# One shared, block-by-block transpose of the attention weights P in a two-stream diffusion block

## The chip, the cores and the metric

The kernel runs on one core of a Trainium2 chip. Its time is the device time of one execution in microseconds (us). Matrix products and transposes run on TensorE (PE in the profile, with its weight loads as PEld), row-wise arithmetic on VectorE (DVE) and ScalarE (ACT), some small work and DMA issues on GpSimd (POOL), and most DMA issues on SyncE (SP). TensorE writes its results to PSUM, and DVE and ACT move them from there to SBUF.

## The reference

Two batches (B = 2) have 256 image tokens and 32 text tokens each, with width D = 1152. Both streams are normalised, scaled and shifted by rows made from `c`; then follow q, k, v products with weights of their own, one attention over the joined 288 tokens of a batch, an output product, a gate and a residual:

```
hi = _layernorm(x_img) * (1 + sci) + shi          # ht the same with the text weights
qi, ki, vi = split(hi @ wqkv_img)                 # qt, kt, vt = split(ht @ wqkv_txt)
q = concat([qt, qi]); k = concat([kt, ki]); v = concat([vt, vi])
scores = einsum('bqd,bkd->bqk', q, k) * D ** -0.5
p = softmax(scores)
a = einsum('bqk,bkd->bqd', p, v)                  # at = a[:, :32], ai = a[:, 32:]
out_i = x_img + gai * (ai @ wo_img)
out_t = x_txt + gat * (at @ wo_txt)
```

## The kernel before

The order on each engine is the order in which the kernel writes its instructions (`keep_in_program_order`), so what stands first in the code is queued first. Semaphores between the engines are placed by the framework. The last third of the kernel, with which the change has to do, runs as follows.

**Scores and softmax.** For each batch and each 128-row image query tile there is one score tile of 128 x 288 (queries x keys, image keys in columns 0 to 255, text keys in 256 to 287). The text queries of both batches share one tile of 64 rows: rows 0 to 31 are batch 0, rows 32 to 63 batch 1. `soft_max`, `soft_exp` and `soft_div` turn a score tile into P, which DVE writes in bf16 into `pb` (L604). A `pb` tile is 384 columns wide. GpSimd writes a second copy of the 32 text-key columns at columns 320 to 351 (L605), so that after the transpose the text keys stand in more than one 32-row group; unused columns are zero.

**Transposes.** The product with V needs P with the keys on the partitions. `p_transposes` (L628) lets PE transpose 128 x 128 pieces of `pb` into a PSUM tile `pT_ps`, and one copy per PSUM tile brings them to `pT` in SBUF. There are three key blocks `kj`: 0 and 1 are image keys, 2 holds the text keys. Each batch has its own `pT`, of 3 x 288 columns. Each batch transposes its two image query tiles and also the shared text tile; for batch 1 a second permutation matrix, `ident2`, puts batch 1's text queries in front. That is 3 pieces x 3 key blocks x 2 batches = 18 transposes. `pT_ps` comes from the PSUM pool `ps_tr` (2 buffers) for the image key blocks and from `ps_mm` (6 buffers) for the text block. The order is: batch 0 blocks 0 and 1 (one ACT copy of 576 columns), batch 0 block 2 (DVE copy of 288), batch 1 block 2 (DVE copy of 288), batch 1 blocks 0 and 1 (ACT copy of 576). DVE also has `v_txt_out` (L519, L521), which finishes the text rows of V, ahead of its two copies.

**Attention.** `attn_pair` is called three times, each time with three 128-wide column blocks of D for each batch. It takes three accumulators of 128 x 288 for batch 0 (t0) and three for batch 1 (t1) from the six `ps_mm` buffers. `attn_keys` adds the two image key blocks for t0, then six short products with the 32 text keys go to t0 and t1 in turn, then `attn_keys` adds the image key blocks for t1. `attn_evac` (L652 on DVE, L654 on ACT, in turn) adds a bias and writes `aT`. In `attn_keys` the loop is by accumulator: key blocks 0 and 1 of one accumulator, then the next accumulator.

**Output.** `out_img` multiplies `aT` with `w_o_i` in chunks of 384 columns, one `ps_mm` buffer each; DVE multiplies by the gate rows `gb` (L719) and adds the residual (L720). `gb` comes by way of DRAM: ACT copies the gate rows to SBUF (L538), POOL issues a write to a scratch tensor (L540), and then a load that spreads it over 128 partitions (L554). POOL's L540 stands behind L605 in POOL's queue.

Of the kernel before, what the change touches and what calls it, by code (L numbers as in the profile page):

```python
# [9 lines left out]
ALU = mybir.AluOpType  # L10
# [4 lines left out]
def kernel(  # L15
# [14 lines left out]
    nc = tc.nc  # L30
    bf = mybir.dt.bfloat16
# [3 lines left out]
    B, NI, D = x_img.shape  # L35
    NT = x_txt.shape[1]
    P = 128
    KT = D // P
    NTOK = NI + NT
    NIT = (B * NI) // P  # L40
    TPB = NI // P
# [10 lines left out]
    const = ctx.enter_context(tc.tile_pool(name="const", bufs=1))  # L52
    work = ctx.enter_context(tc.tile_pool(name="work", bufs=2))
    small = ctx.enter_context(tc.tile_pool(name="small", bufs=4))
    ps_mm = ctx.enter_context(tc.tile_pool(name="ps_mm", bufs=6, space=PSUM))
    ps_tr = ctx.enter_context(tc.tile_pool(name="ps_tr", bufs=2, space=PSUM))

    pin = tc.keep_in_program_order

    def mm(*a, **k):  # L60
        return pin(nc.tensor.matmul(*a, **k))  # L61

    def tr(*a, **k):
        return pin(nc.tensor.transpose(*a, **k))  # L64
# [63 lines left out]
    ident = const.tile([P, P], bf)  # L128
# [13 lines left out]
    PBW = 3 * P  # L142
# [5 lines left out]
    nc.gpsimd.memset(pb_txt, 0.0)  # L148
    nc.gpsimd.memset(xn_t[NTT:P, (KT - KH) * P:KH * P], 0.0)
    nc.gpsimd.memset(pb_all[:, 0:2 * B, NTOK:PBW], 0.0)  # L150
    ident2 = const.tile([P, P], bf)
    nc.gpsimd.tensor_copy(ident2[:, 0:P - NT], ident[:, NT:P])
    nc.gpsimd.tensor_copy(ident2[:, P - NT:P], ident[:, 0:NT])
    fold = const.tile([P, NGG, LW], bf)
    nc.vector.reduce_max(fold[:, 0, :], ident[:].rearrange("p (g l) -> p l g", g=NGG), axis=AX.X)
    nc.gpsimd.tensor_copy(fold[:, 1:NGG, :], fold[:, 0, :].unsqueeze(1).to_broadcast([P, NGG - 1, LW]))
# [120 lines left out]
    v_i = act.tile([P, NIT, D], bf, tag="A")  # L277
# [83 lines left out]
    for kt in range(KT):  # L361
        for b in range(B):
            h = hT_i[:, kt, b * NI:(b + 1) * NI]
            if b == 0 or kt % 3 == 0:
                nc.vector.tensor_scalar(h, h, sc1_i[:, kt, b:b + 1], sh_i[:, kt, b:b + 1],
                                        op0=ALU.mult, op1=ALU.add)
# [141 lines left out]
    def v_txt(r):  # L508
        ps = ps_mm.tile([P, VC], f32, tag="mm")
        for kt in range(KT):  # L510
            for g in range(2):
                for b in range(B):
                    c0, r0 = g * HD + r * VC, 64 * g + NT * b
                    mm(ps[r0:r0 + NT, :], lhsT=hT_t[:, kt, NT * b:NT * b + NT], rhs=w_v_t[:, kt, c0:c0 + VC],
                       start=(kt == 0), stop=(kt == KT - 1), tile_position=(0, r0))
        return ps

    def v_txt_out(r, ps):
        pin(nc.vector.tensor_sub(v_t[:, r * VC:(r + 1) * VC], ps[:], svb[:, r * VC:(r + 1) * VC]))  # L519
        if r == 0:  # L520
            pin(nc.vector.tensor_sub(v_t[0:NTT, HD:HD + NTT], ps[NTT:P, 0:NTT], svb[NTT:P, 0:NTT]))  # L521
# [30 lines left out]
    def img_gate_spread():  # L552
        for b in range(B):
            pin(nc.gpsimd.dma_start(gb[:, b, :], gsc[0, b, :].partition_broadcast(P)))  # L554
        for g in range(2):
            pin(nc.gpsimd.dma_start(xf[64 * g:64 * g + NTT, :, :],
                                    xt_flat.rearrange("t (r g j) -> g t r j", r=2, g=2)[g]))
# [24 lines left out]
    qpos = [[0, P, 2 * P], [NT, NT + P, 0]]  # L582

    pbs = {}
# [15 lines left out]
    def soft_div(key):  # L600
        sps, qn, nmx, e, rs = soft[key]
        pin(nc.vector.reciprocal(rs[0:qn, :], rs[0:qn, :]))  # L602
        pb = pb_txt if key == "t" else pb_tiles[key[0] * TPB + key[1]]
        pin(nc.vector.tensor_scalar_mul(pb[0:qn, 0:NTOK], e[0:qn, :], rs[0:qn, :]))  # L604
        pin(nc.gpsimd.tensor_scalar(pb[0:qn, NI + 2 * NT:NI + 3 * NT], e[0:qn, NI:NTOK], rs[0:qn, :], 0.0,  # L605
                                     op0=ALU.mult, op1=ALU.add))
        pbs[key] = pb

    def scores_img(b, qi):
# [13 lines left out]
                   start=(ft < 2), stop=(ft >= KT - 2), tile_position=(0, r0))  # L623
        return sps

    pTs = {}

    def p_transposes(b, kjs, pool, copy):  # L628
        pT_ps = pool.tile([P, 8 * P], bf, tag="tr" if pool is ps_tr else "mm", name="pT_ps")
        txt = [(2, pbs["t"], ident2 if b else ident)]  # L630
        img = [(qi, pbs[(b, qi)], ident) for qi in range(TPB)]
        for n, kj in enumerate(kjs):
            for qi, pb, perm in (txt + img if b else img + txt):
                o = n * NTOK + qpos[b][qi]
                k0 = kj * P - (NT * b if kj == 2 else 0)
                tr(pT_ps[:, o:o + P], pb[:, k0:k0 + P], perm[:])
        if b not in pTs:
            pTs[b] = work.tile([P, 3, NTOK], bf, tag="pT", name="pT")
        pin(copy(pTs[b][:, kjs[0]:kjs[-1] + 1, :],  # L639
                 pT_ps[:, 0:len(kjs) * NTOK].rearrange("p (k n) -> p k n", n=NTOK)))  # L640

    def attn_keys(tiles, first):
        for b, dt in tiles:
            for kj in range(2):
                mm(tiles[(b, dt)][:], lhsT=v_i[:, b * TPB + kj, dt * P:(dt + 1) * P], rhs=pTs[b][:, kj, :],
                   start=(first and kj == 0), stop=(not first and kj == 1))

    def attn_evac(tiles):
        for b, dt in tiles:
# [7 lines left out]
    def attn_pair(ids0, ids1):  # L657
        t0 = {key: ps_mm.tile([P, NTOK], f32, tag="mm", name="aps") for key in ids0}
        attn_keys(t0, True)
        t1 = {key: ps_mm.tile([P, NTOK], f32, tag="mm", name="aps") for key in ids1}  # L660
        for n, key in enumerate([x for pair in zip(t0, t1) for x in pair]):
            first, (b, dt) = key in t1, key
            r0, vcols = v_txt_cols(b, dt)
            mm((t1 if first else t0)[key][:], lhsT=vcols,
               rhs=pTs[b][r0:r0 + NT, 2, :], start=first, stop=not first, tile_position=(r0, 0))
        attn_evac(t0)
        attn_keys(t1, False)
        attn_evac(t1)
# [9 lines left out]
    soft_exp(I[0])  # L678
    soft_max(I[1], sp[I[1]], P)
    soft_div(I[0])  # L680
    soft_exp(I[1])
    soft_max(I[2], sp[I[2]], P)
    soft_div(I[1])
    soft_exp(I[2])
    soft_max(I[3], sp[I[3]], P)
    soft_div(I[2])
    pin(nc.scalar.copy(half[:], st[NTT:P, :]))
    soft_exp(I[3])
# [5 lines left out]
    gate_row()  # L694
    v_txt_out(0, vt[0])
    vt.append(v_txt(1))
    p_transposes(0, (0, 1), ps_tr, nc.scalar.copy)
    v_txt_out(1, vt[1])
    p_transposes(0, (2,), ps_mm, nc.vector.tensor_copy)
    p_transposes(1, (2,), ps_mm, nc.vector.tensor_copy)  # L700
    p_transposes(1, (0, 1), ps_tr, nc.scalar.copy)
    img_gate_spread()
    for dts in ((0, 5, 1), (6, 2, 7), (3, 8, 4)):
        attn_pair(*[[(b, dt) for dt in dts] for b in range(B)])
# [73 lines left out]
```

## Time and profile before

| what | value |
|---|---|
| median of 5 runs | 117.56 us (117.33, 117.47, 117.56, 117.80, 118.17) |
| profiled execution | 117.33 us |
| its span in the profile | 115.5 us |
| PE busy | 110.8 us (96%), 1081 matmuls and transposes |
| DVE / ACT / POOL busy | 72.0 / 44.1 / 12.4 us |
| granted TensorE clock | 1.0 |

Times inside the profile count from the start of the span. The profiled execution is 1.8 us longer than its span, and what lies around the span is taken as unchanged. In a group of instructions the columns are line, engine, operation, output<-inputs, shapes and count, then busy time and mean duration of one in ns, then idle time of the engine before them and what ended it. In a timeline a row is start, duration, engine, line, operation, output<-inputs, count, and in brackets the idle time before it; several equal instructions in a row are merged.

### The profile page before, as it was taken

The numbers are of one execution on the slowest core, as the hardware profiler recorded it, in microseconds if no ns is written. First come the engines' busy times: TensorE is split into PE (matmuls) and PEld (weight loads), VectorE is DVE, ScalarE is ACT, GpSimd is POOL, SyncE is SP. The second block draws the span as 40 slices with busy tenths as digits, with TensorE's granted clock in tenths as the row PEclk, the third lists the DMA queues.
The fourth block names the chain that finished last, engine by engine and source line by source line (L and its number), as shares of the span: only waits on it lengthen the run. The fifth ranks groups of instructions, "written<-read, shape, count | busy, mean of one in ns | idle before, by whom it ended". The sixth has DMA issues, their size and how long they took to land.

```text
span 115.5 us, 2586 instructions
## 1 busy us (share of the span) xinstructions
PE 110.8 (96%) x1081; PEld 63.5 (55%) x1081; DVE 72.0 (62%) x152; ACT 44.1 (38%) x92; POOL 12.4 (11%) x34
## 2 busy tenths in 40 slices
PE   4999999999999999999999999999999999999990
PEld 1246644445674444445454457887866556656670
DVE  3479691072959999999995040028758509566571
ACT  5799800050852389735241233334557400100000
POOL 7300000000000000000000000003431600416000
PEclk9999999999999999999999999999999999999999
DMA  3999999999999999999999999999999999952223
GB/s 104 379 385 382 392 404 412 412 413 411 412 397 412 312 396 403 414 410 412 410 364 391 412 405 410 414 407 409 416 402 407 405 417 373 407 190 50 103 51 102
DMA packets 18917, 41.02 MB, mean 355 GB/s; under 512 B 1323, under 2 KB 1851, under 8 KB 18907
## 3 DMA queue, kind: packets, MB, share of 16 engines
q1 hardware_dynamic: 18032, 39.85, 89.9%
q0 software_dynamic: 480, 0.89, 2.2%
q10 hardware_dynamic: 395, 0.12, 0.5%
q8 instruction: 8, 0.13, 0.4%
q14 instruction: 2, 0.02, 0.0%
HBM read 39.52 MB, written 1.34 MB: 354 GB/s over the span
## 4 chain that ended last, share of the span: by engine, by line
PE 83%; DMA 9%; SPq 2%; DVE 2%; ACT 1%; issue 0%
PE ps L61 53%; PE vps L61 15%; DMA t<-in_wqkv_img_dram 9%; PE gps L61 5%; PE aps L61 5%; PE sps L61 4%; SPq L108 2%; DVE tmp L719 1%; DVE o L720 1%; SPq L104 1%; ACT pT L639 1%; PE pT_ps L64 0%; PE tpt L64 0%; PE shps L61 0%
## 5 line engine op out<-in xcount | busy, mean ns | idle before, releaser
L61 PE MATMUL ps<-xT_i,t 128*128 128x512 bf16 x162 | 35.7, 379 | 0.0
L61 PEld LDWEIGHTS <-t 128*128 128x128 bf16 x333 | 20.9, 98 | 19.2 <-issue 0.7
L453 DVE SCALAR_TENSOR_TENSOR acc_sh<-t,sTf,acc_sh 128x1152 f32<-128x1152 bf16 x16 | 21.4, 1404 | 0.0
L61 PE MATMUL ps<-t,aT 128*128 128x384 bf16 (+3 forms) x153 | 20.3, 308 | 0.0
L61 PE MATMUL vps<-t,hS_i 128*128 128x512 bf16 (+1 forms) x108 | 17.9, 326 | 0.1
L61 PEld LDWEIGHTS <-aT 128*128 128x128 bf16 (+1 forms) x153 | 13.0, 101 | 7.1 <-issue 0.8
L61 PEld LDWEIGHTS <-hS_i 128*128 128x128 bf16 x108 | 8.9, 98 | 8.9 <-DVE hS_i L272 0.6
L383 ACT CAST qkT<-ps 128x512 bf16<-128x512 f32 (+2 forms) x11 | 6.1, 551 | 14.8 <-PE ps L61 13.5
L719 DVE TENSOR_TENSOR tmp<-ps,gb 128x384 bf16<-128x384 f32 (+2 forms) x13 | 6.8, 525 | 7.5 <-PE ps L61 3.8
L605 POOL TENSOR_SCALAR pb<-e,rs 128x32 bf16<-128x32 f32 (+1 forms) x5 | 2.2, 445 | 75.5 <-DVE rs L602 75.5
L61 PE MATMUL wps<-warm 128*128 128x512 bf16 x24 | 8.2, 505 | 1.5 <-DVE unit L127 1.5
L381 ACT ACTIVATE qkT<-ps 128x512 bf16<-128x512 f32 (+2 forms) x11 | 6.0, 559 | 8.3 <-PE ps L61 6.7
L180 DVE CAST v_i<-vps 128x512 bf16<-128x512 f32 x5 | 3.5, 691 | 7.9 <-PE vps L61 7.9
L590 DVE TENSOR_REDUCE nmx<-sps 128x1 f32<-128x288 f32 x4 | 1.8, 458 | 9.4 <-PE sps L61 9.4
L182 ACT CAST v_i<-vps 128x512 bf16<-128x512 f32 x4 | 2.3, 580 | 10.0 <-PE vps L61 10.0
L61 PEld LDWEIGHTS <-warm 128*128 128x128 bf16 x25 | 2.7, 119 | 5.5 <-issue 3.0
L652 DVE TENSOR_SCALAR aT<-aps,svc 128x288 bf16<-128x288 f32 x9 | 4.3, 518 | 2.2 <-PE aps L61 2.2
L61 PEld LDWEIGHTS <-sT 128*32 128x32 bf16 x180 | 4.5, 96 | 1.8 <-issue 1.2
L61 PE MATMUL sps<-qkT 128*128 128x288 bf16 (+1 forms) x54 | 5.3, 287 | 0.0
L61 PE MATMUL gps<-t,sT 128*32 128x288 bf16 x144 | 5.2, 287 | 0.0
L61 PE MATMUL aps<-pT,v_i 128*128 128x288 bf16 x36 | 5.1, 287 | 0.1
L61 PE MATMUL ps<-hT_t,t 128*128 128x64 bf16 x162 | 5.0, 193 | 0.0
(114 smaller groups left out, 105.6 us busy)
## 6 DMA issues: line engine op xcount, KB each, us to landing
t<-in_wqkv_txt_dram SPq DMA_DIRECT2D x3, 2592.0 KB, 20.1
t<-in_wmod_img_dram SPq DMA_DIRECT2D x2, 2592.0 KB, 14.3
t<-in_wmod_txt_dram SPq DMA_DIRECT2D x2, 2592.0 KB, 19.7
t<-in_wqkv_img_dram SPq DMA_DIRECT2D x3, 864.0 KB, 13.5
t<-in_wqkv_img_dram SPq DMA_DIRECT2D x1, 2592.0 KB
t<-in_wo_img_dram SPq DMA_DIRECT2D x3, 864.0 KB, 10.9
t<-in_wqkv_img_dram SPq DMA_DIRECT2D x3, 576.0 KB, 10.5
t<-in_wmod_txt_dram SPq DMA_DIRECT2D x2, 864.0 KB, 13.0
```

The source lines that it names most:

```text
L61: return pin(nc.tensor.matmul(*a, **k))
L104: nc.sync.dma_start(x_i[:, b * TPB:(b + 1) * TPB, :], x_img[b].rearrange("(p t) d -> p t d", t=TPB))
L108: nc.sync.dma_start(w_sc_i[:, r0:r1, :], sc_v[:, r0:r1, :])
L180: nc.vector.tensor_copy(out_ap, in_ap)
L182: nc.scalar.copy(out_ap, in_ap)
L381: nc.scalar.mul(out_ap, in_ap, SCALE)
L383: nc.scalar.copy(out_ap, in_ap)
L453: pin(nc.vector.scalar_tensor_tensor(acc, w_sh_t[:, kt, :], col, acc, op0=ALU.mult, op1=ALU.add))
L590: pin(nc.vector.reduce_max(nmx[0:qn, :], sps[0:qn, :], axis=AX.X, negate=True))
L605: pin(nc.gpsimd.tensor_scalar(pb[0:qn, NI + 2 * NT:NI + 3 * NT], e[0:qn, NI:NTOK], rs[0:qn, :], 0.0, op0=ALU.mult, op1=ALU.add))
L652: nc.vector.tensor_scalar(dst, tiles[(b, dt)][:], bias, None, op0=ALU.add)
L719: nc.vector.tensor_mul(tmp[:, 0:n], ps[:, 0:n], gb[:, b, c0:c0 + n])
```

## The change

The text tile is transposed once for both batches. One `pT` of 3 x 576 columns holds both: batch 0's two image tiles, batch 0's text, batch 1's text, batch 1's image tiles. A PSUM tile now holds one key block for both batches, so there are three of them (blocks 0 and 1 from `ps_tr`, block 2 from `ps_mm`) and 15 transposes, ordered by key block, all with `ident`. `ident2` goes. For the text tile GpSimd writes its text-key columns three times over (64 x 96 in place of 64 x 32). All 15 transposes are queued ahead of the copies: ACT copies block 0 of batch 0, block 1 of batch 0 and block 1 of batch 1 (288 columns each); DVE copies block 0 of batch 1 (288) and then block 2 of both batches (576). On the t0 side `attn_keys` now goes by key block: block 0 of all three accumulators, then block 1 of all three.

```diff
-    ident2 = const.tile([P, P], bf)
-    nc.gpsimd.tensor_copy(ident2[:, 0:P - NT], ident[:, NT:P])
-    nc.gpsimd.tensor_copy(ident2[:, P - NT:P], ident[:, 0:NT])
...
-        pin(nc.gpsimd.tensor_scalar(pb[0:qn, NI + 2 * NT:NI + 3 * NT], e[0:qn, NI:NTOK], rs[0:qn, :], 0.0,
-                                     op0=ALU.mult, op1=ALU.add))
+        if key == "t":
+            dst, src = pb[0:qn, NTOK:PBW].rearrange("p (r k) -> p r k", k=NT), \
+                e[0:qn, NI:NTOK].unsqueeze(1).to_broadcast([qn, PBW // NT - NTOK // NT, NT])
+        else:
+            dst, src = pb[0:qn, NI + 2 * NT:NI + 3 * NT], e[0:qn, NI:NTOK]
+        pin(nc.gpsimd.tensor_scalar(dst, src, rs[0:qn, :], 0.0, op0=ALU.mult, op1=ALU.add))
...
-    pTs = {}
-    def p_transposes(b, kjs, pool, copy):
-        pT_ps = pool.tile([P, 8 * P], bf, tag="tr" if pool is ps_tr else "mm", name="pT_ps")
-        txt = [(2, pbs["t"], ident2 if b else ident)]
-        img = [(qi, pbs[(b, qi)], ident) for qi in range(TPB)]
-        for n, kj in enumerate(kjs):
-            for qi, pb, perm in (txt + img if b else img + txt):
-                o = n * NTOK + qpos[b][qi]
-                k0 = kj * P - (NT * b if kj == 2 else 0)
-                tr(pT_ps[:, o:o + P], pb[:, k0:k0 + P], perm[:])
-        if b not in pTs:
-            pTs[b] = work.tile([P, 3, NTOK], bf, tag="pT", name="pT")
-        pin(copy(pTs[b][:, kjs[0]:kjs[-1] + 1, :],
-                 pT_ps[:, 0:len(kjs) * NTOK].rearrange("p (k n) -> p k n", n=NTOK)))
+    pT = work.tile([P, 3, B * NTOK], bf, tag="pT", bufs=1, name="pT")
+    pTs = [pT[:, :, b * NTOK:(b + 1) * NTOK] for b in range(B)]
+    def p_transposes(kj, pool):
+        ps = pool.tile([P, B * NTOK], bf, tag="tr" if pool is ps_tr else "mm", name="pT_ps")
+        k0 = kj * P
+        for pb, c0, o in [(pbs[(0, qi)], k0, qpos[0][qi]) for qi in range(TPB)] + [(pbs["t"], k0, NI)] + \
+                [(pbs[(1, qi)], k0 - (NT if kj == 2 else 0), NTOK + qpos[1][qi]) for qi in range(TPB)]:
+            tr(ps[:, o:o + P], pb[:, c0:c0 + P], ident[:])
+        return ps
+    def p_out(kj, ps, copy, b0=0, b1=B):
+        pin(copy(pT[:, kj, b0 * NTOK:b1 * NTOK], ps[:, b0 * NTOK:b1 * NTOK]))

     def attn_keys(tiles, first):
-        for b, dt in tiles:
-            for kj in range(2):
-                mm(tiles[(b, dt)][:], ...)
+        loop = [(kj, key) for kj in range(2) for key in tiles] if first else \
+            [(kj, key) for key in tiles for kj in range(2)]
+        for kj, (b, dt) in loop:
+            mm(tiles[(b, dt)][:], ...)
...
     vt.append(v_txt(1))
-    p_transposes(0, (0, 1), ps_tr, nc.scalar.copy)
+    pt0, pt1, pt2 = p_transposes(0, ps_tr), p_transposes(1, ps_tr), p_transposes(2, ps_mm)
     v_txt_out(1, vt[1])
-    p_transposes(0, (2,), ps_mm, nc.vector.tensor_copy)
-    p_transposes(1, (2,), ps_mm, nc.vector.tensor_copy)
-    p_transposes(1, (0, 1), ps_tr, nc.scalar.copy)
+    p_out(0, pt0, nc.scalar.copy, 0, 1)
+    p_out(0, pt0, nc.vector.tensor_copy, 1, B)
+    p_out(1, pt1, nc.scalar.copy, 0, 1)
+    p_out(2, pt2, nc.vector.tensor_copy)
+    p_out(1, pt1, nc.scalar.copy, 1, B)
     img_gate_spread()
```

More of the change, by code (lines that the diff above doesn't have):

```diff
@@ L624, in scores_txt @@
         return sps
-    pTs = {}
-    def p_transposes(b, kjs, pool, copy):
-        pT_ps = pool.tile([P, 8 * P], bf, tag="tr" if pool is ps_tr else "mm", name="pT_ps")
-        txt = [(2, pbs["t"], ident2 if b else ident)]
-        img = [(qi, pbs[(b, qi)], ident) for qi in range(TPB)]
-        for n, kj in enumerate(kjs):
-            for qi, pb, perm in (txt + img if b else img + txt):
-                o = n * NTOK + qpos[b][qi]
-                k0 = kj * P - (NT * b if kj == 2 else 0)
-                tr(pT_ps[:, o:o + P], pb[:, k0:k0 + P], perm[:])
-        if b not in pTs:
-            pTs[b] = work.tile([P, 3, NTOK], bf, tag="pT", name="pT")
-        pin(copy(pTs[b][:, kjs[0]:kjs[-1] + 1, :],
-                 pT_ps[:, 0:len(kjs) * NTOK].rearrange("p (k n) -> p k n", n=NTOK)))
-    def attn_keys(tiles, first):
-        for b, dt in tiles:
-            for kj in range(2):
-                mm(tiles[(b, dt)][:], lhsT=v_i[:, b * TPB + kj, dt * P:(dt + 1) * P], rhs=pTs[b][:, kj, :],
-                   start=(first and kj == 0), stop=(not first and kj == 1))
+    pT = work.tile([P, 3, B * NTOK], bf, tag="pT", bufs=1, name="pT")
[9 more added lines that the diff above has]
+        pin(copy(pT[:, kj, b0 * NTOK:b1 * NTOK], ps[:, b0 * NTOK:b1 * NTOK]))
+    def attn_keys(tiles, first):
+        loop = [(kj, key) for kj in range(2) for key in tiles] if first else \
+            [(kj, key) for key in tiles for kj in range(2)]
+        for kj, (b, dt) in loop:
+            mm(tiles[(b, dt)][:], lhsT=v_i[:, b * TPB + kj, dt * P:(dt + 1) * P], rhs=pTs[b][:, kj, :],
+               start=(first and kj == 0), stop=(not first and kj == 1))
     def attn_evac(tiles):
```

## The prediction

> **What bounds the kernel now.** I read the busy times first, then the chain of waits that ended last, and then the timeline where that chain leaves PE. PE is busy for 110.8 of 115.5 us, and DMA and the other engines appear on the chain only at its two ends and once in the middle:
>
> ```profile
> PE 110.8 (96%) x1081; PEld 63.5 (55%) x1081; DVE 72.0 (62%) x152; ACT 44.1 (38%) x92; POOL 12.4 (11%) x34
> ```
>
> The chain in order of time (start, length, what) shows that middle place. PE makes the first six transposes, ACT copies them, and only then does the attention product start:
>
> ```profile
> 83.95 0.46 PE pT_ps L64 x6
> 84.41 0.02 issue
> 84.43 0.65 ACT pT L639
> 85.08 0.04 issue
> 85.12 5.94 PE aps L61 x54
> 91.06 5.85 PE ps L61 x36
> 96.91 1.22 PE gps L61 x36
> 98.12 12.79 PE ps L61 x99
> ```
>
> From 85.12 PE is on the chain without a break to 110.91, so what the first attention product gains should reach the end, if nothing else is late. The change touches nothing else on the chain. The timeline of this stretch:
>
> ```profile
> 83.05 0.46 POOL L605 TENSOR_SCALAR pb<-e,rs 64x32 bf16<-64x32 f32 x1 [0.37 <-DVE rs L602]
> 83.89 1.18 PE L64 MATMUL pT_ps<-ident,pb 128*128 128x128 bf16 x18
> 84.01 0.46 DVE L519 TENSOR_TENSOR v_t<-ps,svb 128x288 bf16<-128x288 f32 x1
> 84.43 1.31 ACT L639 COPY pT<-pT_ps 128x576 bf16<-128x576 bf16 x2 [1.39 <-PE pT_ps L64]
> 84.60 0.52 DVE L639 COPY pT<-pT_ps 128x288 bf16<-128x288 bf16 x2
> 85.12 0.90 PE L61 MATMUL aps<-pT,v_i 128*128 128x288 bf16 x6
> 85.95 0.42 PE L61 MATMUL aps<-pT,v_t 32*128 32x288 bf16 x6
> 86.30 1.64 PE L61 MATMUL aps<-pT,v_i 128*128 128x288 bf16 x12
> ```
>
> The 18 transposes start (1.18 - 0.22) / 17 = 0.056 us apart (0.22 is the length of one). The last one starts at about 84.85, and PE then has nothing until 85.12. So the change can win two things: three transposes (3 x 0.056 = 0.17 us), and the rest of the wait for ACT (85.12 - 84.91 = 0.21 us), 0.38 us together. It can't win more, because after 85.12 PE waits for none of it.
>
> **When ACT can start.** Before, its first copy waited for six transposes: 83.89 + 5 x 0.056 + 0.22 = 84.39, and it started at 84.43, 0.04 later. In the changed program it waits for the five of block 0: 84.34, so it starts at 84.38.
>
> **How long the first copy takes.** It has 288 columns in place of 576. The trace has no ACT copy of this size from bf16 PSUM, but it has neighbours on both sides:
>
> ```profile
> L639 ACT COPY pT<-pT_ps 128x576 bf16<-128x576 bf16 x2 | 1.3, 638 | 1.4 <-PE pT_ps L64 1.4
> L441 ACT COPY xT_t<-tpt 128x320 bf16<-128x320 bf16 x1 | 0.4, 432 | 0.0
> L441 ACT COPY xT_t<-tpt 128x256 bf16<-128x256 bf16 x1 | 0.4, 392 | 0.0
> ```
>
> 288 lies midway between 256 and 320, so I take 0.41 us (0.39 to 0.43). The copy ends at 84.79. Before, the copy ended at 84.43 + 0.64 = 85.07 and PE began at 85.12, 0.05 later. So the first attention product moves to 84.84, **0.28 us earlier**. PE's own queue allows that: 15 transposes are issued by 83.89 + 15 x 0.056 = 84.73.
>
> **What could hold PE after that.** Five things have to be in time.
>
> *ACT's second copy (block 1 of batch 0).* Its ten transposes end at 83.89 + 9 x 0.056 + 0.22 = 84.61. The two L441 copies above run back to back in 0.71 us, so the second began 0.11 before the first ended. The second copy therefore starts at 84.68 to 84.79 and is with PE at 84.68 + 0.41 + 0.05 = 85.14 to 85.25. PE's six products at 85.12 start (0.90 - 0.29) / 5 = 0.12 apart, and the new order by key block puts three of them on block 0, so PE wants block 1 at 84.84 + 0.37 = 85.21. The stall is 0 to 0.04. In the old order by accumulator PE would want it after one product, at 84.96, and would wait 0.2.
>
> *DVE's two copies.* `v_txt_out` ends at 84.47 and DVE is free, but the built program makes its copy of block 0 wait for ACT's copy from the same PSUM tile. The trace has such a pair of readers: DVE's transpose L225 reads the tile that ACT's L405 reads.
>
> ```profile
> 34.10 0.40 ACT L405 CAST svr<-gps 128x288 bf16<-128x288 f32 x1 [1.17 <-PE gps L61]
> 34.53 0.48 DVE L225 STREAM_TRANSPOSE svc<-gps 128x288 f32<-128x288 f32 x1 [0.97 <-ACT svr L405]
> ```
>
> DVE sat idle for 0.97 us and started 0.03 after ACT ended. So I count the two copies of block 0 in sequence: DVE starts at 84.83. Its next copy, of 576 columns, has no row of its size; DVE copies from bf16 PSUM are 302 ns for 288 columns (L639, two in 0.52, so 0.22 from start to start) and 555 ns for 768 (L260). By a straight line 576 takes 0.30 + 0.25 x 288 / 480 = 0.45; the upper bound is two copies of 288, 0.60. It starts at 84.83 + 0.22 to 0.30 = 85.05 to 85.13, and PE can use it at 85.55 to 85.63 (up to 85.78 with 0.60). PE wants it for the first text product, which stood 0.83 after the first key product (85.95 - 85.12), so at 85.67. No stall by the line; 0.03 to 0.11 by the upper bound. Behind this copy on DVE stand only the `aT` evictions, which need those text products anyway.
>
> The Trainium skill, "PSUM — Partial Sum Buffer", section "PSUM bank collisions raise a hardware error", says that two engines must not access one bank on the same partitions at once, reads against reads included; it speaks against splitting one tile's copy between ACT and DVE, and the L405 and L225 rows show software obeying it. Without that rule DVE could copy at 84.47 and the text block would be ready some 0.1 us sooner, but PE would still be last, so the sum is the same by both.
>
> *GpSimd's wider text multiply.* The 64x32 one took 0.46 us. The 64x96 one lies between that and three times as much, 1.38, because a 128x32 one also takes 0.36 to 0.47 and a POOL copy of 96 columns takes 258 ns against 200 for 32 (L152, L153). I take 0.55. It ends between 83.51 and 84.43. The text transpose of block 2 is the 13th, at 83.89 + 12 x 0.056 = 84.56, so the cover is 0.13 even at the upper end. Behind it in POOL's queue stand the two scratch writes L540 and then the `gb` loads, which land up to 0.92 later. The wait list has "DVE tmp L719 <- DMA gb<-mod_scratch: 3.6": DVE resumes at 95.25, or 96.17 at worst. PE feels that only when it needs the first of the six `ps_mm` buffers again, for the last chunk of the second output tile at 99.5 before and 99.2 now. DVE gives that buffer back 0.56 after it resumes, at 96.73 at the latest. The cover is 2.5 us, so the cost is nothing. The removed `ident2` copies (0.26 and 0.20 us at 2.92 to 3.33 on POOL) save nothing either: POOL waits afterwards for DVE's `sT` until 5.45.
>
> *The accumulators of the next group.* By key block, PE asks for the third t0 buffer after 2 x 0.12 = 0.25 us and no longer after 0.49. ACT's second eviction (L654: three in 1.28 us from 86.28, mean 498) ends at about 87.17 and PE can go 0.05 later, at 87.22. PE's first product of the next group is at 86.30 + 6 x 0.12 = 87.04, so it now asks at 87.29. That leaves 0.07, and all these times move together; cost nothing, but the margin was 0.31.
>
> *Alternating accumulators.* In the V product PE changes its accumulator at most steps, in the image q and k products it stays for nine. The chain has them at 13.76 / 63 = 0.218 and 19.53 / 90 = 0.217 us each. The alternation costs nothing.
>
> ACT's third copy ends by 85.6 and is wanted at 86.0. The weights for the output product are not on the chain.
>
> **Sum.** 0.28 less a stall of 0 to 0.04 at block 1, and less up to 0.11 at the text block: 0.17 to 0.28, and I take 0.27. The profiled execution would go from 117.33 to 117.06. That execution lies 0.23 under the median of 117.56, so against the median I say **117.29 us**. The gain is 0.23%. About 0.5% (0.59 us) is what a measurement of this kernel can tell from no change, and the five times of before spread over 0.84 us.
>
> **Rivals.** *The gain is lost behind PE* (117.56 on the median). Then something in the output stage that doesn't move with PE would decide the end. For it speaks that DVE waits for `gb` until 95.25 whatever PE does; against it speak the buffers above, 3.7 us of cover before the change, and that the chain names only PE from 85.12 to 110.91. Chance 0.14.
>
> *The slower one: GpSimd's text multiply is late.* If the operand read three times over costs far more than its columns, the 13th transpose waits, and the text products with it: from the end of the multiply it takes 0.05, two more transposes (0.11), 0.22, 0.04, DVE's 0.45 and 0.05, together 0.92 us. It decides once the text products come later than 85.95, that is when the multiply ends after 85.03 and takes 1.98 us, 4.3 times the 64x32 row. At six times (2.76 us, twice the cost of three separate multiplies) text products start at 86.73, 0.78 late, and the median is 118.34. No row of POOL's suggests it: fixed cost rules in all its small operations. Chance 0.14, which also takes in a price of this kind at the other shortened margins.
>
> *DVE becomes the last.* The text block is ready at 86.0 or so where its copy and the wait for ACT both stretch; the gain is 0 to 0.17 and the time 117.4 to 117.56. Chance 0.12. My forecast has the remaining 0.60.
>
> **The range.** From below: all of 0.38 on the lowest of the runs is 117.33 - 0.38 = 116.95, and I go 0.1 lower for another set of runs, 116.85. From above: the rival without gain on the slower runs of before, and a mild form of the slower rival, 118.05. The chances: the forecast with its 0.23% lies within 0.5% by itself, but medians of five of so wide a spread move by some tenths of a per cent, so of its 0.60 I give 0.22 to faster by over 0.5% and 0.37 to within, 0.01 to slower. The lost gain: 0.02, 0.11, 0.01. DVE last: 0.02, 0.09, 0.01. The slower rival: 0.11 slower, 0.03 within. Together faster 0.26, within 0.60, slower 0.14.
>
> **What would show it.** In the profile of the changed kernel: 15 transposes from 83.9; the first ACT copy of 288 columns at 84.38 for 0.41 us; the first key product at 84.84, six of them 0.12 apart with no gap after the third; DVE's first copy only after ACT's, at 84.83, and its second for 0.45; POOL's text multiply ended before 84.5; text products at 85.67; the chain from there on as before, 0.27 earlier. Wrong would be a gap on PE ahead of block 1 or of the text products, PE waiting for an eviction between groups, or a chain that leaves PE in the output stage.

## The result and the profile after

The changed kernel takes 117.47 us (median of 33 runs, 117.17 to 118.03), the kernel before 117.84 us (median of 59, 117.31 to 118.50). The ratio is 0.997 with a 95% interval of 0.9959 to 0.998: a gain of 0.3% (0.24 to 0.48 us by the interval), clear of zero and under the 0.5% that the prediction called "within". The forecast was 0.23% and 117.29 us; the time lies in the stated range of 116.85 to 118.05.

The profiled execution of the changed kernel has a span of 115.2 us (115.5 before). Line numbers differ a little from before: L516 is the old L519, L607 the old L605, L721 the old L719. The end of the chain of waits of the changed kernel, in order of time (start, length, what):

```profile
83.99 0.94 PE pT_ps L64 x15
84.93 5.87 PE aps L61 x54
90.80 5.85 PE ps L61 x36
96.65 1.22 PE gps L61 x36
97.86 12.79 PE ps L61 x99
```

ACT's copy (0.65 us of the chain before) is not named in it, and every piece behind the attention product has the length that it had. This doesn't mean that PE no longer waits for the copy. The transposes are listed until 84.93, which is after the first product's start at 84.86 in the rows below, so the chain finds no idle time of PE to put down to ACT, and its piece of 5.87 begins 0.07 late (90.80 - 84.86 is 5.94, as before). By the single instructions, counted from the first transpose, ACT's first copy ended at 1.184 before and ends at 0.889 now, and the first product starts 0.052 us after that end both times. The timeline of the same kernel for the stretch that the prediction worked on:

```profile
83.08 0.52 POOL L607 TENSOR_SCALAR pb<-e,rs 64x96 bf16<-64x96 f32 x1 [0.37 <-DVE rs L599]
83.92 1.01 PE L64 MATMUL pT_ps<-ident,pb 128*128 128x128 bf16 x15
84.05 0.46 DVE L516 TENSOR_TENSOR v_t<-ps,svb 128x288 bf16<-128x288 f32 x1
84.41 1.00 ACT L639 COPY pT<-pT_ps 128x288 bf16<-128x288 bf16 x3 [1.33 <-PE pT_ps L64]
84.84 0.67 DVE L639 COPY pT<-pT_ps 128x288 bf16<-128x288 bf16 x2 [0.34 <-ACT pT L639]
84.86 0.90 PE L61 MATMUL aps<-pT,v_i 128*128 128x288 bf16 x6
85.69 0.42 PE L61 MATMUL aps<-pT,v_t 32*128 32x288 bf16 x6
86.04 1.64 PE L61 MATMUL aps<-pT,v_i 128*128 128x288 bf16 x12
```

From the first transpose to the first key product it was 85.12 - 83.89 = 1.23 us before (1.236 unrounded) and is 84.86 - 83.92 = 0.94 now. The six key products keep the length of 0.90, so there is no gap between key blocks. The twelve products across the border of the first two groups keep 1.64, so the accumulators of the next group, for which the prediction saw a margin of 0.07 us, cost nothing. The rest is best told by one more pair of times, from the first transpose to the first output product (90.90 before, 90.64 after): 7.01 and 6.72. The whole difference of 0.295 us arises before the first key product and is kept to the end. The whole runs agree with it within their scatter: their medians differ by 0.37 us, and the mean span is 115.71 us in 35 runs of the kernel before and 115.40 in 34 of the changed one, a difference of 0.31.

### The profile page after: what moved, and what is told of

It reads as the page before. It is cut to its first block, busy times and chain, and to the rows that moved or that the text cites. A ratio compares the mean times of both kernels' runs of the same rounds, so it can differ in the third digit from the quotient of the medians.

```text
span 115.2 us, 2579 instructions
## 1 busy us (share of the span) xinstructions
PE 110.3 (96%) x1078; PEld 63.4 (55%) x1078; DVE 72.2 (63%) x152; ACT 43.9 (38%) x93; POOL 12.1 (10%) x32
## 4 chain that ended last, share of the span: by engine, by line
PE 84%; DMA 9%; SPq 2%; DVE 2%; issue 0%
PE ps L61 53%; PE vps L61 15%; DMA t<-in_wqkv_img_dram 9%; PE gps L61 5%; PE aps L61 5%; PE sps L61 4%; SPq L108 2%; DVE tmp L721 1%; PE pT_ps L64 1%; DVE o L722 1%; SPq L104 1%; PE tpt L64 0%; PE shps L61 0%
## 5 line engine op out<-in xcount | busy, mean ns | idle before, releaser
L721 DVE TENSOR_TENSOR tmp<-ps,gb 128x384 bf16<-128x384 f32 (+2 forms) x13 | 6.8, 525 | 7.7 <-DMA gb<-mod_scratch 3.9
L607 POOL TENSOR_SCALAR pb<-e,rs 128x32 bf16<-128x32 f32 (+1 forms) x5 | 2.3, 456 | 75.5 <-DVE rs L599 75.5
```

What stands on the lines that cost most here:

```text
L607: pin(nc.gpsimd.tensor_scalar(dst, src, rs[0:qn, :], 0.0, op0=ALU.mult, op1=ALU.add))
L721: nc.vector.tensor_mul(tmp[:, 0:n], ps[:, 0:n], gb[:, b, c0:c0 + n])
```

## The experiments

All of them are read by the same four points in time, each counted from the start of the first transpose (us, from the single instructions of each trace, which the timelines shown here merge):

| kernel | first key product | first text product | first output product | end of DVE's work | median of runs |
|---|---|---|---|---|---|
| before | 1.236 | 2.064 | 7.010 | 31.59 | 117.84 (59) |
| changed | 0.941 | 1.768 | 6.715 | 31.29 | 117.47 (33) |
| whole copies | 1.180 | 2.008 | 6.953 | 31.53 | 117.80 (12) |
| split only, 18 transposes | 1.016 | 1.847 | 6.793 | 31.37 | 117.57 (12) |
| keys by accumulator | 0.941 | 1.948 | 6.894 | 31.47 | 117.64 (12) |
| DVE copies first | 0.856 | 1.706 | 6.655 | 31.23 | 117.52 (12) |
| no wait of DVE for ACT | 0.941 | 1.768 | 6.715 | 31.29 | one run |
| three text multiplies | 0.940 | 1.768 | 6.715 | 31.29 | one run |

The ratios given below compare an experiment with 35 runs of the kernel before that were taken along with it (median 117.79). Each ratio's interval is some 0.5% wide, 0.6 us, which is more than any of the effects looked for; so the stretches decide, and the medians only have to agree.

**Do the stretches repeat?** Differences of a tenth of a microsecond are smaller than the scatter of whole executions, so both kernels were profiled once more.

The changed kernel again:

> The changed kernel once more. Theory: an execution differs from another before the first transpose only (83.9 to 84.4 so far), and the stretch from there repeats: 0.94 to the first key product, 6.72 to the first output product, 31.29 to the end of DVE's work, within 0.02. Rival (the stretch itself scatters): differences of 0.1 or more, and the comparison of stretches proves little.

It gave 0.940, 6.713 and 31.295. The kernel before again:

> The kernel before once more. Theory: 1.24, 7.01 and 31.59 again within 0.02, whatever the time of the execution. Rival: differences of 0.1 or more.

It gave 1.236, 7.009 and 31.587. The stretches repeat within 0.01 us, while the first transpose started anywhere from 83.87 to 84.40 us in the ten profiles. On these two pairs, a difference of 0.05 us between two stretches can be believed; a difference of 0.1 us between two medians of twelve runs can't.

**Fewer transposes without the split copies.** The copies are whole again:

```diff
     v_txt_out(1, vt[1])
-    p_out(0, pt0, nc.scalar.copy, 0, 1)
-    p_out(0, pt0, nc.vector.tensor_copy, 1, B)
-    p_out(1, pt1, nc.scalar.copy, 0, 1)
+    p_out(0, pt0, nc.scalar.copy)
+    p_out(1, pt1, nc.vector.tensor_copy)
     p_out(2, pt2, nc.vector.tensor_copy)
-    p_out(1, pt1, nc.scalar.copy, 1, B)
```

> The 15 transposes and the order by key block stay; the copies are no longer by batch halves (ACT takes all 576 columns of block 0, DVE all of block 1 and then block 2). Measured in the profile from the first transpose: to the first key product it was 1.24 us before and 0.94 after; to the first output product 7.01 and 6.72. Theory (the length of the first ACT copy sets the gain, and fewer transposes by themselves give nothing): ACT starts 0.49 after the first transpose, takes 0.64, PE follows 0.05 later: 1.18 and 6.95, so nearly all of the gain is lost and the time is 0.24 us above the changed kernel. Rival (three fewer transposes are most of the gain, 0.17 us): 1.07 and 6.84, the time 0.12 us above the changed kernel.

Timeline of this kernel:

```profile
84.31 1.01 PE L64 MATMUL pT_ps<-ident,pb 128*128 128x128 bf16 x15
84.80 0.64 ACT L639 COPY pT<-pT_ps 128x576 bf16<-128x576 bf16 x1 [1.32 <-PE pT_ps L64]
85.48 0.90 PE L61 MATMUL aps<-pT,v_i 128*128 128x288 bf16 x6 [0.17 <-ACT pT L639]
```

1.180 and 6.953, as the theory had it (1.18 and 6.95), not the rival's 1.07 and 6.84. PE now finishes its transposes early and waits for ACT (the bracket on the last row). Of the 0.295 us only 0.057 is left, because ACT may start after five transposes in place of six. Its ratio to the kernel before is 1.0001 (0.9976 to 1.0025): whole runs show no gain.

**The split copy without fewer transposes.** The kernel before, with its 18 transposes (shortened; ... stands for what is left out):

```diff
-        pin(copy(pTs[b][:, kjs[0]:kjs[-1] + 1, :], ...))
+        for n0, n1 in ([(n, n + 1) for n in range(len(kjs))] if b == 0 else [(0, len(kjs))]):
+            pin(copy(pTs[b][:, kjs[n0]:kjs[n1 - 1] + 1, :], ...))
...
     def attn_keys(tiles, first):
+        loop = [(kj, key) for kj in range(2) for key in tiles] if first else ...
```

> The kernel before with its 18 transposes, but ACT copies the two key blocks of batch 0 one by one (288 columns each) and the first key products go by key block. Theory: ACT starts 0.55 after the first transpose and takes 0.41, PE could start at 1.01, but the 18 transposes are issued only by 18 x 0.056 = 1.01 and PE needs a little more to change over: 1.02 to 1.10 to the first key product, 6.79 to 6.88 to the first output product, so 0.13 to 0.22 us better than before and 0.08 to 0.16 short of the changed kernel. Rival (fewer transposes are the gain): at most 0.1 better than before, 6.91 or more.

Timeline of this kernel:

```profile
83.92 1.18 PE L64 MATMUL pT_ps<-ident,pb 128*128 128x128 bf16 x18
84.46 1.31 ACT L640 COPY pT<-pT_ps 128x288 bf16<-128x288 bf16 x3 [1.38 <-PE pT_ps L64]
84.93 0.90 PE L61 MATMUL aps<-pT,v_i 128*128 128x288 bf16 x6
```

1.016 and 6.793: just under the theory's 1.02 to 1.10, and far from the rival's 6.91 or more. ACT's copy ended 0.945 after the first transpose, so with the 0.052 that PE needed after a copy's end in the other kernels it could have started at 0.997; the 18th transpose started at 0.960 and the product followed 0.056 later, one transpose's step. Here PE itself is the bound, and the change from transposes to products costs nothing extra. So the split copy with its new order alone is worth 0.22 us, the 15 transposes alone 0.06, and both together 0.295. Behind the split, the 15 transposes bring 0.08 of the 0.17 us that they take off PE; then ACT's copy, which ends at 0.889, is the bound again. The ratio is 0.999 (0.9961 to 1.0018), which by itself shows no gain.

**Key products by accumulator.**

```diff
-        loop = [(kj, key) for kj in range(2) for key in tiles] if first else \
-            [(kj, key) for key in tiles for kj in range(2)]
+        loop = [(kj, key) for key in tiles for kj in range(2)]
```

> The changed kernel, but the first key products go by accumulator as before (block 0 and 1 of one accumulator, then the next). Theory: PE wants block 1 0.12 after the first product, at 1.06 from the first transpose, and ACT's second copy is with it only at 1.24: a gap of 0.18 after the first key product, first output product at 6.89, 0.18 us above the changed kernel. Rival (the order makes no difference, since text products or DVE's copy come last anyway): 6.72.

Timeline of this kernel:

```profile
84.40 1.01 PE L64 MATMUL pT_ps<-ident,pb 128*128 128x128 bf16 x15
84.89 1.00 ACT L639 COPY pT<-pT_ps 128x288 bf16<-128x288 bf16 x3 [1.33 <-PE pT_ps L64]
85.34 1.07 PE L61 MATMUL aps<-pT,v_i 128*128 128x288 bf16 x6
```

The six key products now take 1.07 us and not 0.90, and the gap stands after the first of them: the second starts 1.242 after the first transpose, 0.30 after the first and not 0.12. That is 0.052 after ACT's second copy ended (1.190), so PE waits for this copy. The first output product comes at 6.894: 0.18 lost, to the hundredth of what was expected, and not the rival's 6.72. Without the new order the changed kernel would gain 0.116 us and not 0.295. The ratio is 0.9986 (0.9962 to 1.001).

**Does the new wait of DVE for ACT cost anything?** ACT takes DVE's half as well:

```diff
     p_out(0, pt0, nc.scalar.copy, 0, 1)
-    p_out(0, pt0, nc.vector.tensor_copy, 1, B)
     p_out(1, pt1, nc.scalar.copy, 0, 1)
     p_out(2, pt2, nc.vector.tensor_copy)
+    p_out(0, pt0, nc.scalar.copy, 1, B)
     p_out(1, pt1, nc.scalar.copy, 1, B)
```

> The changed kernel, but ACT takes all four image halves (block 0 of batch 0, block 1 of batch 0, block 0 of batch 1, block 1 of batch 1), so DVE copies only block 2 and no longer waits for ACT's read of the same PSUM tile. Theory (DVE's wait is covered: its last copy ended 1.59 after the first transpose and the text products start at 1.77): text products at 1.77 and first output product at 6.72 as in the changed kernel; DVE's copy begins at about 1.05 as the transposes of block 2 end. Rival (DVE's wait costs PE): text products up to 0.1 earlier.

Timeline of this kernel:

```profile
84.21 1.01 PE L64 MATMUL pT_ps<-ident,pb 128*128 128x128 bf16 x15
85.26 0.46 DVE L639 COPY pT<-pT_ps 128x576 bf16<-128x576 bf16 x1 [0.46 <-PE pT_ps L64]
85.98 0.42 PE L61 MATMUL aps<-pT,v_t 32*128 32x288 bf16 x6
```

DVE's copy of block 2 started 1.05 after the first transpose and ended at 1.51, 0.09 earlier than in the changed kernel, and PE used it at 1.768 all the same. The wait exists and is covered.

**Does the price that the prediction feared on GpSimd matter?** The text multiply as three of 64x32 in place of one of 64x96 (the added lines, shortened):

```diff
+        for c0 in ((NTOK, NTOK + NT, NTOK + 2 * NT) if key == "t" else (NI + 2 * NT,)):
+            pin(nc.gpsimd.tensor_scalar(pb[0:qn, c0:c0 + NT], e[0:qn, NI:NTOK], rs[0:qn, :], 0.0, ...))
```

> The changed kernel, but the text multiply of GpSimd is three of 64x32 in place of one of 64x96, the price that the prediction took as the upper bound. Theory: POOL ends near 0.4 to 0.55 after the first transpose, before the 13th transpose wants it at 0.68; the transposes, the text products (1.77) and the first output product (6.72) stay; the gate rows land up to 0.9 later, and the end does not move against the first output product. Rival (the slower one of the prediction): transposes of block 2 late, text products after 1.77.

Timeline of this kernel, GpSimd alone:

```profile
83.36 0.98 POOL L603 TENSOR_SCALAR pb<-e,rs 64x32 bf16<-64x32 f32 x3 [0.37 <-DVE rs L599]
84.29 1.33 POOL L537 DMA_DIRECT2D mod_scratch<-g_sb  x2
89.74 1.13 POOL L551 DMA_DIRECT2D gb<-mod_scratch  x2 [4.13 <-DMA mod_scratch<-g_sb]
```

Nothing moved on PE: 0.940, 1.768, 6.715. The size expected for the multiplies was too high: the three took 0.98 us together (0.46, then 0.28 each as they follow each other) and ended 0.15 after the first transpose, not at 0.4 to 0.55, while the first text transpose of block 2 is due at 0.68. The loads of `gb`, which stand behind the multiplies in GpSimd's queue, were issued 0.43 later than in the changed kernel, counted from the first transpose (89.74 - 84.19 against 89.04 - 83.92), and the end stayed at 31.29. One run, read by its stretches.

**Is there more to have in the same place?** DVE's copy of 288 columns takes 0.31 us and ACT's 0.40, so DVE takes the first one and finishes V's text rows afterwards:

```diff
+    p_out(0, pt0, nc.vector.tensor_copy, 0, 1)
     v_txt_out(1, vt[1])
-    p_out(0, pt0, nc.scalar.copy, 0, 1)
-    p_out(0, pt0, nc.vector.tensor_copy, 1, B)
     p_out(1, pt1, nc.scalar.copy, 0, 1)
+    p_out(0, pt0, nc.scalar.copy, 1, B)
     p_out(2, pt2, nc.vector.tensor_copy)
     p_out(1, pt1, nc.scalar.copy, 1, B)
```

> The changed kernel, but DVE takes the first copy (block 0 of batch 0, 288 columns, 0.30 us there and 0.40 on ACT) and finishes the text rows of V behind it; ACT takes block 1 of batch 0, block 0 and block 1 of batch 1. Theory (the first copy still sets the start): the first key product comes at 0.49 + 0.30 + 0.05 = 0.84 from the first transpose if PE can do it; its 15 transposes are issued by 0.84 to 0.85, so 0.85 to 0.91, and 6.62 to 6.69 to the first output product, 0.03 to 0.1 us under the changed kernel. Rival (PE's change from transposes to products needs the 0.15 us that it shows now): no change, 0.94 and 6.72. A loss would show as a wait for block 1 or for the text block.

Timeline of this kernel:

```profile
84.19 1.01 PE L64 MATMUL pT_ps<-ident,pb 128*128 128x128 bf16 x15
84.68 0.31 DVE L639 COPY pT<-pT_ps 128x288 bf16<-128x288 bf16 x1 [0.41 <-PE pT_ps L64]
85.05 0.91 PE L61 MATMUL aps<-pT,v_i 128*128 128x288 bf16 x6
85.39 0.45 DVE L639 COPY pT<-pT_ps 128x576 bf16<-128x576 bf16 x1
```

0.856 and 6.655: 0.06 us under the changed kernel, and the rival (0.94) falls. Two bounds meet here: the 15th transpose started at 0.793, and one step of 0.056 later is 0.849; DVE's copy ended at 0.798, and 0.052 later is 0.850. This run can't tell which of them held PE; by these numbers a still shorter copy would gain next to nothing. The text products come 0.85 after the first key product and not 0.83, since DVE's copy of block 2 ends only at 1.653 and PE follows 0.053 later, at 1.706; so 0.02 of the 0.085 is given back. Its ratio to the kernel before is 0.9975 (0.9951 to 0.9998). By the stretch it beats both kernels, the changed one by 0.06 us; its twelve runs (117.52) can't be told from the changed kernel's (117.47).

## Why the prediction was right, step by step

| step | predicted, from the first transpose | measured |
|---|---|---|
| ACT starts | 0.49 | 0.490 |
| its copy of 288 columns | 0.41 (0.39 to 0.43) | 0.399 |
| first key product | 0.95 | 0.941 |
| stall at key block 1 | 0 to 0.04 | 0 |
| DVE's first copy starts, after ACT's | 0.94 | 0.921 |
| DVE's copy of 576 columns | 0.45 (up to 0.60) | 0.448 |
| text products | 1.78 | 1.768 |
| GpSimd's wide multiply | 0.55 (0.46 to 1.38) | 0.515 |
| gain | 0.27 (0.17 to 0.28) | 0.295 |

The mechanism was the one named: a shorter first copy that starts one transpose earlier. The whole-copies run shows it by taking the split away, and the split-only run shows the bound behind it. The gain in the stretch came out just above the stated 0.17 to 0.28: ACT's copy was 0.01 shorter than the middle of its neighbours, the 0.01 taken off for a stall at key block 1 wasn't needed, and the rest is rounding. ACT's second copy started 0.295 after the first, 0.10 before it ended, and ended at 1.190; PE could use it at 1.242, as the run by accumulator shows, and wanted it at 1.306. The prediction had these two at 1.25 to 1.36 and at 1.32.

The prediction's upper bound for the gain, 0.38 us, agrees with the runs: with the first key product one step behind the 15th transpose, as in the split-only run behind the 18th, it comes at 0.849, which is 0.387 earlier than before. The kernel in which DVE copies first reached 0.380 there and kept 0.355 to the first output product.

*The lost gain.* It was given 0.14 and didn't happen. DVE resumed at 95.30 after its wait for `gb`, 0.05 later in the span than before (95.25), while PE was 0.26 earlier. The wait list of the changed kernel:

```profile
DVE tmp L721 <- DMA gb<-mod_scratch: 3.9, 1, 3.9
```

It grew from 3.6 to 3.9, and none of it reached the end: DVE's last work is 0.30 us earlier than before, counted from the first transpose.

*The slower rival and DVE as the last.* They were given 0.14 and 0.12, and each was tried by itself: with three multiplies nothing moved on PE, and without the wait for ACT nothing moved there either. The slower rival needed a multiply of 1.98 us; the one of 64x96 took 0.515, and even three of 64x32 took 0.98, not the 1.38 that the prediction set as the upper end.

*What was off* is the level, not the difference. The five runs of before had a median of 117.56; the 59 now have 117.84. The prediction went from the former, so its 117.29 is 0.18 under the measured 117.47 although the gain was under-told. These two errors go against each other by luck: the level was 0.28 low, and by the medians the gain was told 0.10 too small. And "what lies around the span is taken as unchanged" holds for medians only (2.17 us in the 35 runs of before, 2.14 in the 34 of the changed kernel): in single runs the time outside the span lay between 1.74 and 2.31 us, and the profiled executions have 1.82 before and 2.18 after. The profiled execution of the changed kernel was therefore not faster (117.42 against 117.33) while its span was 0.27 shorter. Why the time outside the span differs from run to run stays open.

## What to carry to other kernels

Where the busiest engine waits once for a chain of "produce, copy, consume", as PE does here, it is the first piece of the copy that counts: split it so that the consumer can start on the first piece, and order the consumer so that it has enough work before it wants the second (three products here, 0.37 us against one copy of 0.40 that overlaps its predecessor). Less work on the producer paid less here (0.06 us alone and 0.08 behind the split, of the 0.17 that it took off PE), because the copy stayed or became the bound; do the two alone as well as together before crediting either. Where whole runs scatter by more than the effect, compare a stretch between two named instructions, and profile the same kernel twice to see how well it repeats.

## What the runs showed that was not expected

From the first transpose to the end of DVE's work, 31.3 us, both kernels repeat within 0.01 us. All the scatter of whole executions that the profiles show lies before it (the first transpose at 83.87 to 84.40 us) and outside the span (1.74 to 2.31 us over all runs).

Small operations that follow each other on one engine start sooner than their listed durations say: ACT's copies of 0.40 us start 0.295 and 0.290 apart, DVE's copy of 0.31 is followed after 0.225, and GpSimd's second and third multiply are listed at 0.28 where the first has 0.46. The sum of the listed durations overstates such a chain: by a fifth for ACT's three copies (1.22 against 1.00 us from start to end), by a quarter for the four of the run without DVE's wait (1.66 against 1.31), but by only 0.04 us for the three multiplies (1.02 against 0.98).
